# A new order for the first unit, a late q load by the software queue, and q loads behind the k transfers

## The chip, the cores and the metric

The kernel runs on one NeuronCore of a Trainium2 chip. Its engines run side by side, each with its own list of instructions: TensorE (PE; the loading of weights into it is listed as PEld), VectorE (DVE), ScalarE (ACT), GpSimd (POOL) and SyncE (SP, which here only issues transfers). An instruction waits until the semaphores of its operands have been raised; what stands behind it in the same list waits too. Transfers issued by SyncE go through a hardware queue, those issued by GpSimd through a software queue; both are carried by the same 16 DMA engines. The metric is the time of one execution on the device in microseconds (us). The kernel before takes 222.96 us, the median of 13 runs (221.85 to 223.95).

## The reference: what is computed

Sparse attention, followed by a two-layer feed-forward. There are 4 batches of 8 heads with 768 positions and a head size of 64. Each position attends to the 31 positions around it and to one summary per block of 32 positions: the largest k of the block as its key, the mean v as its value.

```python
k_sum = k.reshape(B, H, nb, block, D).max(axis=3)
v_sum = v.reshape(B, H, nb, block, D).mean(axis=3)
scores_l = where(|pos_i - pos_j| < 16, scale * q @ k.T, -1e9)
scores_s = scale * q @ k_sum.T + log(block)
a = softmax(concat([scores_l, scores_s]))
attn = a @ concat([v, v_sum])
h = x @ w_in                      # x: attn as [3072, 512]; w_in [512, 2048]
out = (h / (1 + exp(-1.702 * h))) @ w_out      # w_out [2048, 512]
```

Inputs and output are float32; the kernel computes in bfloat16 with float32 sums in PSUM.

## The kernel before

**Units.** The work is cut into 8 units `u`: a batch `b = u // 2` and half of its positions (384). A unit is attention for its half, a transposition of the result to `xT[0..3]` (one tile for each pair of heads `p`), then `ff_in` (16 column tiles `nt` of h, four matmuls each, a gelu on ACT into `gT`) and `ff_out` (3 blocks `ms` of 128 rows, each in 4 parts of 4 matmuls, copied by ACT and stored). The attention of unit u + 1 is written between the parts of ff_out of unit u: `beside(u + 1, i)` looks up in `plan`, `plan0` or `plan1` what goes to slot i (s: scores of a pair, v: values, t: transposition of q on TensorE, x: of the result on TensorE, d: of the result by a transfer).

**Order.** Every engine keeps the order in which the program writes its instructions (`_Ordered`). For the first unit, which has no ff_out to stand beside, this order is written out by hand as a list of short steps (from `cast_k(act, 0, 0)` on); the engine is an argument of most steps. For a pair p:

- `cast_k`, `cast_q` bring the float32 load to bfloat16; `k_turn`, `q_turn` transpose it on TensorE (products with `ident`) into PSUM; `k_own`, `q_copy` bring it from there to `kx` and `qT`.
- `k_max` takes the block maxima, `k_blocks` puts them into `ksz`, `k_sides` copies neighbouring keys.
- `s_turn`, `s_exp`, `s_mask` give the local weights `a_sb`; `b_turn`, `b_exp` those of the summaries (`ab`, two pairs in one tile).
- `v_own`, `v_even`, `v_before`, `v_after` put v into `vw`; `v_sum` and `v_copy` make the block sums.
- `av_near`, `av_blocks` form the values in PSUM, `v_norm` divides, `x_turn` transposes; a `copy` brings the result to `xT[p]`; `ff_first(p)` does the products of xT[p] for the first `N0 = 2` column tiles.
- `idle(n)` issues n matmuls on the constant tile `warm`, whose result nobody reads. They go to unused columns of the tile that `st["idle"]` names at that point: that of the last k_turn, s_turn, av_near or v_copy.

"dve_alone" as an engine means a copy by a reduction over an axis of length one.

**PSUM.** Two pools share its 8 banks: `pmm` (4 tiles of one bank) and `psb` (2 tiles of two banks), each handed out in turn. A tile is handed out again when the last reader of its predecessor is done.

**Queues.** SyncE first issues the loads of batch 0: k (8 transfers), the first half of q (4), v (8), the second half of q (4; "late q", first needed by `cast_q(dve, p, 1)` at the start of ff_in of unit 0, whose `q_turn(p, 1)` stand behind nt = 4 to 7). GpSimd issues the weights, cast to bfloat16 on the way, in 8 chunks: `load_w_in(0)` and `(1)` inside the list, the other six after it. In ff_out of unit 0 SyncE issues `hold`, a small transfer that reads the third w_out chunk, and behind it all loads of batch 1. Batches 2 and 3 are loaded in ff_out of units 1 and 3: k at `i == 1`, v and q at `i == 8` (i counts parts, and is raised before it is compared). In units 2 and 4 GpSimd casts the next batch; k and q are then transposed by transfers: `xk` at the start of the unit, `xq` in its ff_out at `i == 10`, followed by `halo_dmas` and `sum_dmas`, which complete `vw`.

Of the kernel before, what the change touches and what calls it, by code (L numbers as in the profile page):

```python
# [9 lines left out]
F32 = mybir.dt.float32  # L10
# [24 lines left out]
def kernel(  # L35
# [45 lines left out]
    raw = {}  # L81
# [16 lines left out]
    def load_q(b, p, half=None):  # L98
# [5 lines left out]
        t = stage.tile([128, 2, JH, D], F32, name=f"qf{p}{half}", tag=f"qf{p}{half}")  # L104
# [3 lines left out]
        raw["q", p, half] = t  # L108
# [206 lines left out]
    def idle(n):  # L315

        tile, o, start = st["idle"]
        for i in range(n):
            pe.matmul(out=tile[:, o:o + 120], lhsT=warm[:, 0:128], rhs=warm[:, 0:120],
                      start=start, stop=True, skip_group_check=True)  # L320
# [63 lines left out]
    st = {}  # L384

    def k_turn(p):
        src = cast.pop(("k", p))
        big = st["K", p] = psb.tile([128, 1024], F32, name="ps_k", tag="big")
        st["idle"] = big, 904, True
# [30 lines left out]
    def q_turn(p, half=0):  # L420
# [6 lines left out]
        for r in range(JH):  # L427
            pe.matmul(out=ps[:, r * 128:r * 128 + 128],
# [3 lines left out]
    def q_copy(p, eng, half=0):  # L432

        copy(eng, qT[p][0][:, half * HALF:half * HALF + HALF].rearrange("p (c r) -> p r c", r=JH),
             st["Q", p][:, 0:HALF].rearrange("p (r c) -> p r c", r=JH))

    def s_turn(p):
# [3 lines left out]
        st["idle"] = big, 904, True  # L441
# [28 lines left out]
    def b_exp(g):  # L470
        ab = st["ab", g] = attp.tile([128, HALF], BF16, name="ab", tag="ab")
        act.activation(out=ab, in_=st["B", g][:, 0:HALF], func=ACT.Exp, scale=scale)

# [25 lines left out]
    def v_copy(p, eng):  # L499
# [4 lines left out]
        if p == NP - 1:  # L504
            st["idle"] = st["VT"], 0, True
# [5 lines left out]
    def av_near(p):  # L511
# [11 lines left out]
        if p < 2:  # L523
            st["idle"] = st["V", p // 2], p % 2 * 512 + 392, False
# [15 lines left out]
    def x_turn(p):  # L540
        src = x_sb.pop(p)
        if p == 0:
            st["X", 0] = pmm.tile([128, 2, HALF], BF16, name="ps_x", tag="mm")
# [123 lines left out]
    N0 = 2  # L667
# [56 lines left out]
    for p in range(NP):  # L724
        load_q(0, p, 1)
# [6 lines left out]
    cast_k(act, 0, 0)  # L732
    cast_k("dve_alone", 0, 1)
    cast_k(act, 1, 1)
    cast_k(pool, 2, 1)
    cast_k(dve, 1, 0)
    k_turn(0)
    k_own(0, dve)
    cast_k(act, 2, 0)
    idle(5)  # L740
    k_turn(1)
    idle(5)
    k_turn(2)
    k_max(0)
    k_own(1, act)
    k_sides(0, dve)
    cast_k(act, 3, 0)
    k_own(2, act)
    k_blocks(0, pool)
    cast_k(dve, 3, 1)  # L750
    k_sides(1, pool)
    k_sides(2, pool)
    k_max(1)
    cast_q(pool, 2, 0)
    cast_q(act, 0, 0)
    idle(4)
    k_turn(3)
    cast_q("dve_alone", 1, 0)
    k_max(2)
    idle(2)  # L760
    q_turn(0)
    k_own(3, act)
    k_sides(3, dve)
    k_blocks(1, pool)
    q_turn(1)
    q_copy(0, act)
    cast_q(pool, 3, 0)
    q_copy(1, act)
    q_turn(2)
    k_blocks(2, pool)  # L770
    idle(3)
    b_turn(0)
    v_own(0, 0, act)
    s_turn(0)
    s_turn(1)
    v_before(0, pool)
    k_max(3)
# [240 lines left out]
```

## Time and profile before

| what | value |
|---|---|
| median of 13 runs | 222.96 us |
| the profiled execution's own time | 222.92 us |
| its span, first to last instruction | 221.2 us |
| TensorE busy | 210.6 us |
| ScalarE busy | 136.8 us |
| VectorE busy | 90.8 us |
| GpSimd busy | 67.9 us |
| moved by the DMA engines | 37.36 MB |
| first ff matmul of unit 0 | at 25.22 us |
| first w_out matmul of unit 0 | at 37.34 us |
| first load of batch 1 | at 42.36 us |

Times within the profile are counted from the first instruction. In a timeline each line gives start, length, engine, operation and names, out<-in, then how many instructions were merged and, in brackets, how long the engine had been idle and what ended that. All of the kernel's instructions carry line 27, that of the helper that records them; they are told apart by the names of their tiles: `kb`, `qb` the casts, `ps_k`, `ps_q`, `ps_s`, `ps_b`, `ps_vt`, `ps_av`, `ps_x` the PSUM tiles of the steps above, `ph` and `po` those of ff_in and ff_out. The chain of work that ended last goes back from the last instruction to what released each step.

### The profile page before, as it was taken

How to read it: one execution, taken by the hardware profiler on the slowest of the kernel's cores; microseconds unless marked ns; L12 is line 12 of the kernel's file. 1: busy time of each engine (PE TensorE's matmuls, PEld its weight loads, DVE VectorE, ACT ScalarE, POOL GpSimd, SP SyncE). 2: the span in 40 equal slices, each digit the busy share in tenths (PEclk: the TensorE clock that was granted, in tenths of full speed). 3: DMA queues.
4: the chain of work that ended last, by engine and by line, in shares of the span. 5: the costliest groups of instructions: out<-in, count | busy, mean ns of one | idle time of the engine just before them, and what ended most of it. 6: DMA issues, size and time to landing. Idle time of an engine off the chain costs nothing.

```text
span 221.2 us, 5025 instructions
## 1 busy us (share of the span) xinstructions
PE 210.6 (95%) x1989; PEld 120.0 (54%) x1989; DVE 90.8 (41%) x262; ACT 136.8 (62%) x241; POOL 67.9 (31%) x164
## 2 busy tenths in 40 slices
PE   7778999999999999999999999999999999999993
PEld 3656765456555556454655465545655564556542
DVE  5689890454984720185506200549126001700000
ACT  3488577556578747862788277845786478637420
POOL 5289983023954428610003256600000000000000
PEclk9999999999999999999999999999999999999999
DMA  5999999899999999999989999999723300340012
GB/s 167 315 217 210 216 215 217 150 235 197 252 342 199 235 207 217 224 154 185 183 171 234 207 236 210 216 165 201 140 60 95 122 0 3 83 128 5 0 47 96
DMA packets 94407, 37.36 MB, mean 169 GB/s; under 512 B 78704, under 2 KB 91440, under 8 KB 94384
## 3 DMA queue, kind: packets, MB, share of 16 engines
q1 hardware_dynamic: 90160, 32.85, 73.4%
q0 software_dynamic: 4224, 4.19, 11.6%
q8 instruction: 15, 0.25, 0.5%
q14 instruction: 8, 0.07, 0.1%
HBM read 27.26 MB, written 6.29 MB: 152 GB/s over the span
## 4 chain that ended last, share of the span: by engine, by line
PE 86%; DVE 6%; ACT 4%; issue 1%; ACTq 0%; DVEq 0%
PE po L27 37%; PE ph L27 36%; PE ps_av L27 4%; PE ps_s L27 3%; PE ps_k L27 2%; DVE kx L27 2%; PE ps_w L27 2%; ACT a_sb L27 1%; ACT kx L27 1%; DVE qT L27 1%; PE ps_q L27 1%; PE ps_x L27 1%; DVE ks L27 1%; PE ps_vt L27 1%; DVE a_sb L27 1%
## 5 line engine op out<-in xcount | busy, mean ns | idle before, releaser
L27 PE MATMUL po<-w_out_sb,gT 128*128 128x512 bf16 (+2 forms) x400 | 89.0, 371 | 0.0
L27 PE MATMUL ph<-xT,w_in_sb 128*128 128x384 bf16 x512 | 86.5, 326 | 0.9 <-DVE xT L27 0.6
L27 ACT ACTIVATE gT<-ph 128x384 bf16<-128x384 f32 x128 | 61.5, 490 | 27.5 <-PE ph L27 27.3
L27 PEld LDWEIGHTS <-w_in_sb 128*128 128x128 bf16 x512 | 49.4, 98 | 33.6 <-issue 1.7
L27 PEld LDWEIGHTS <-gT 128*128 128x128 bf16 x400 | 36.4, 98 | 38.5
L27 DVE TENSOR_TENSOR a_sb<-a_sb,mk 128x768 bf16<-128x768 bf16 x32 | 18.9, 597 | 75.1 <-ACT a_sb L27 73.8
L27 ACT ACTIVATE osb<-po 128x512 f32<-128x512 f32 (+1 forms) x24 | 14.2, 592 | 36.6 <-PE po L27 36.6
L27 ACT ACTIVATE a_sb<-ps_s 128x768 bf16<-128x768 f32 x32 | 24.3, 806 | 7.0 <-PE ps_s L27 6.5
L27 POOL CAST vw<-vf 128x768 bf16<-128x768 f32 (+3 forms) x35 | 24.2, 719 | 13.1 <-DMA vf<-in_v_dram 12.6
L27 POOL CAST kb<-kf 128x768 bf16<-128x768 f32 (+1 forms) x13 | 10.7, 820 | 48.8 <-DMA kf<-in_k_dram 48.8
L27 ACT ACT_TABLE_LOAD x16 | 20.5, 1283 | 1.1 <-PEq L1002 0.8
L27 DVE TENSOR_TENSOR x<-ps_av,rc 128x384 bf16<-128x384 f32 x28 | 15.6, 558 | 1.0
L27 POOL CAST qb<-qf 128x384 bf16<-128x384 f32 (+1 forms) x18 | 12.3, 696 | 8.2 <-DMA qf<-in_q_dram 5.6
L27 DVE TENSOR_REDUCE ks<-kx 128x24 bf16<-128x768 bf16 x12 | 11.2, 937 | 1.4 <-ACT kx L27 1.4
L27 PEld LDWEIGHTS <-a_sb 128*64 128x64 bf16 x384 | 8.0, 111 | 6.7 <-issue 3.8
L27 DVE COPY osb<-po 128x128 f32<-128x128 f32 x1 | 0.3, 292 | 24.9 <-PE po L27 24.9
L27 PE MATMUL ps_av<-vw,a_sb 128*64 128x65 bf16 x384 | 10.1, 198 | 0.2 <-DVE a_sb L27 0.2
L27 PEld LDWEIGHTS <-kx 64*128 64x128 bf16 x384 | 7.0, 95 | 4.7 <-issue 4.0
L27 PE MATMUL ps_s<-qT,kx 64*128 64x64 bf16 x384 | 9.2, 191 | 0.4 <-ACT qT L27 0.2
L27 PEld LDWEIGHTS <-warm 128*128 128x128 bf16 x71 | 6.0, 115 | 6.4 <-issue 4.8
L27 DVE COPY kx<-kx 128x80 bf16<-128x80 bf16 (+4 forms) x52 | 8.9, 223 | 0.9 <-ACT kx L27 0.9
L27 DVE CAST qT<-ps_q 128x384 bf16<-128x384 f32 (+1 forms) x8 | 7.6, 961 | 3.3 <-PE ps_q L27 3.2
(70 smaller groups left out, 119.9 us busy)
## 6 DMA issues: line engine op xcount, KB each, us to landing
out_dram<-osb SPq DMA_DIRECT2D x23, 256.0 KB, 2.3
kf<-in_k_dram SPq DMA_DIRECT2D x12, 384.0 KB, 6.6
vf<-in_v_dram SPq DMA_DIRECT2D x12, 384.0 KB, 6.8
qf<-in_q_dram SPq DMA_DIRECT2D x16, 192.0 KB, 4.3
qf<-in_q_dram SPq DMA_DIRECT2D x8, 384.0 KB, 6.2
w_in_sb<-in_moe_w_in_dram POOLq DMA_DIRECT2D x4, 512.0 KB, 9.8
w_out_sb<-in_moe_w_out_dram POOLq DMA_DIRECT2D x4, 512.0 KB, 17.8
kf<-in_k_dram SPq DMA_DIRECT2D x8, 192.0 KB, 3.8
```

The lines of the kernel that those rows point to most:

```text
L27: r = f(*a, **kw)
```

## The change

- The list of the first unit is written in another order, with other engines for many steps.
- `idle` writes 128 columns of `st["idle"]` only once that names a tile: the q tile of the last pair after its q_copy, then the second b tile after its b_exp; before, none are issued. The lines that named other tiles go. `busy` is defined and not called.
- `q_turn` for the first half writes PSUM so that `q_copy` reads it contiguously.
- `N0` is 3.
- Late q of batch 0 becomes one load for all pairs, issued by GpSimd behind the list's end, ahead of `load_w_in(2)`.
- `ff_in(u, range(3))` at the start of a unit holds for units 1 and 2 as well.
- q of batches 2 and 3 is loaded at the start of units 2 and 4, behind `xk`; v at `i == 7`.

```diff
@@ load_q
+        if half and p == 0:
+            late[0] = stage.tile([128, NP, 2, JH, D], F32, name="qfl", tag="qfl")
+            if b == 0:
+                pool.dma_start(out=late[0].rearrange("p i h r d -> p (i h) (r d)"),
+                               in_=q[0, :, HALF:S].rearrange("h (p r) d -> p h (r d)", r=JH))
+        t = (late[0][:, p] if half else
+             stage.tile([128, 2, JH, D], F32, name=f"qf{p}0", tag=f"qf{p}0"))
+        raw["q", p, half] = t
+        if b == 0 and half:
+            return
@@ idle
-        tile, o, start = st["idle"]
+        if st.get("idle") is None:
+            return
         for i in range(n):
-            pe.matmul(out=tile[:, o:o + 120], lhsT=warm[:, 0:128], rhs=warm[:, 0:120],
-                      start=start, stop=True, skip_group_check=True)
+            pe.matmul(out=st["idle"][:, 0:128], lhsT=warm[:, 0:128], rhs=warm[:, 0:128],
+                      start=True, stop=True)
@@ q_turn, q_copy
-            pe.matmul(out=ps[:, r * 128:r * 128 + 128],
+            pe.matmul(out=ps[:, r * 128:r * 128 + 128] if half else at(ps, r, [[JH, 128]]),
...
+        if half == 0:
+            copy(eng, qT[p][0][:, 0:HALF], st["Q", p][:, 0:HALF])
+            if p == NP - 1:
+                st["idle"] = st["Q", p]
+            return
@@ b_exp
+        if g:
+            st["idle"] = st["B", g]
@@ x_turn
+            if st.get("idle") is st["Q", NP - 1]:
+                st["idle"] = None
@@
-    N0 = 2
+    N0 = 3
@@ the list (new order only)
+    cast_k("dve_alone", 0, 0)
+    cast_k(dve, 0, 1)
+    cast_k(dve, 1, 0)
+    cast_k(dve, 1, 1)
+    k_turn(0)
+    cast_k(pool, 2, 1)
+    k_own(0, act)
+    k_turn(1)
+    k_sides(0, dve)
+    cast_k(act, 2, 0)
+    k_own(1, act)
+    k_turn(2)
+    k_max(0)
+    k_blocks(0, dve)
+    k_sides(1, pool)
+    cast_k(act, 3, 0)
+    k_own(2, act)
+    cast_k(dve, 3, 1)
+    k_turn(3)
+    cast_q(pool, 0, 0)
+    k_own(3, act)
+    cast_q(pool, 1, 0)
+    q_turn(0)
+    cast_q(pool, 2, 0)
+    q_copy(0, act)
+    q_turn(1)
+    k_max(1)
+    k_sides(2, pool)
+    q_turn(2)
+    k_max(2)
+    q_copy(1, act)
+    s_turn(0)
+    b_turn(0)
+    k_blocks(2, dve)
+    q_copy(2, act)
+    k_blocks(1, pool)
+    v_own(0, 0, pool)
+    b_turn(1)
+    cast_q(dve, 3, 0)
+    k_max(3)
+    v_before(0, pool)
+    v_own(0, 1, "dve_alone")
+    s_turn(2)
+    s_exp(0)
+    b_exp(0)
+    k_sides(3, pool)
+    q_turn(3)
+    s_exp(2)
+    s_turn(1)
+    v_even(0, dve)
+    s_mask(0, dve)
+    s_exp(1)
+    v_before(1, act)
+    q_copy(3, dve)
+    v_sum(0)
+    v_even(1, act)
+    v_own(1, 0, pool)
+    v_after(0, pool)
+    v_copy(0, dve)
+    b_turn(2)
+    s_turn(3)
+    v_own(1, 1, dve)
+    s_mask(2, dve)
+    idle(8)
+    v_sum(1)
+    s_mask(1, dve)
+    av_near(0)
+    v_after(1, act)
+    k_blocks(3, pool)
+    v_copy(1, act)
+    v_own(2, 0, "dve_alone")
+    av_blocks(0, 0, D + 1)
+    b_turn(3)
+    v_own(2, 1, act)
+    av_near(1)
+    load_w_in(0)
+    load_w_in(1)
+    av_blocks(1, 0, D + 1)
+    v_before(2, pool)
+    b_exp(1)
+    idle(8)
+    v_sum(2)
+    v_own(3, 0, "dve_alone")
+    v_norm(0)
+    v_after(2, pool)
+    v_own(3, 1, "dve_alone")
+    x_turn(0)
+    v_even(2, act)
+    s_exp(3)
+    idle(6)
+    v_sum(3)
+    idle(4)
+    av_near(2)
+    v_copy(2, act)
+    v_after(3, act)
+    copy(dve, xT[0], st["X", 0 // 2][:, 0 % 2])
+    v_norm(1)
+    v_before(3, pool)
+    av_blocks(2, 0, D + 1)
+    s_mask(3, dve)
+    v_even(3, pool)
+    v_copy(3, act)
+    x_turn(1)
+    idle(4)
+    av_near(3)
+    v_norm(2)
+    gelu_soon()
+    copy(act, xT[1], st["X", 1 // 2][:, 1 % 2])
+    idle(4)
+    av_blocks(3, 0, D + 1)
+    idle(8)
+    x_turn(2)
+    ff_first(0)
+    ff_first(1)
+    v_norm(3)
+    x_turn(3)
+    copy(act, xT[2], st["X", 2 // 2][:, 2 % 2])
+    ff_first(2)
+    copy(dve, xT[3], st["X", 3 // 2][:, 3 % 2])
+    ff_first(3)
+    for p in range(NP):
+        load_q(0, p, 1)
     load_w_in(2)
@@ the units
                     xk(p // 2, s)
             for p in range(NP):
+                load_q(b + 1, p)
+            for p in range(NP):
                 cast_v(pool, s, p, 0)
...
-        if u > 2:
+        if u:
             ff_in(u, range(3))
...
-            elif half and b + 2 < B and i == 8:
+            elif half and b + 2 < B and i == 7:
                 load_v(b + 2)
-                for p in range(NP):
-                    load_q(b + 2, p)
```

## The prediction, made before the change was run

> **What bounds the kernel now.** I read the page first, then the chain that ended last, the timeline of the first 45 us engine by engine, and the DMA side (windows, landings, SyncE's waits).
>
> ```profile
> span 221.2 us, 5025 instructions
> PE 210.6 (95%) x1989; PEld 120.0 (54%) x1989; DVE 90.8 (41%) x262; ACT 136.8 (62%) x241; POOL 67.9 (31%) x164
> DMA  5999999899999999999989999999723300340012
> ```
>
> TensorE is the engine that ends last; its 95% contains the idle matmuls of the first unit. The DMA row says the second thing: the transfer engines are as full as TensorE up to slice 28, some 155 us. So time can be won only where TensorE waits, and only as far as the transfers come earlier too. The chain (start, length, what):
>
> ```profile
> 26.76 2.93 PE ph L27 x18
> 32.30 5.20 PE ph L27 x32
> 51.02 0.57 DVE xT L27
> 79.35 0.57 DVE xT L27
> 79.96 10.25 PE ph L27 x62
> ```
>
> From 26.8 us on it is TensorE with short holes; the holes are the copies of xT at 51.0 and 79.4, and the part before 26.8, where the chain changes engine more than twenty times. The timeline of TensorE shows why the first part is slow (in brackets: idle before, and what ended it):
>
> ```profile
> 7.19 0.66 PE L27 MATMUL ps_k<-warm 128*128 128x120 bf16 x5 [1.05 <-DVE kx L27]
> 7.64 1.48 PE L27 MATMUL ps_k<-ident,kb 128*128 128x128 bf16 x6
> 9.43 1.39 PE L27 MATMUL ps_k<-ident,kb 128*128 128x128 bf16 x6
> 11.71 0.37 PE L27 MATMUL ps_k<-warm 128*128 128x120 bf16 x4 [0.90 <-ACT kx L27]
> 11.92 0.82 PE L27 MATMUL ps_k<-ident,kb 128*128 128x128 bf16 x6
> 21.56 0.52 PE L27 MATMUL ps_vt<-vw,E 128*64 128x128 bf16 x6 [0.44 <-DVE vs L27]
> 26.60 3.09 PE L27 MATMUL ph<-xT,w_in_sb 128*128 128x384 bf16 x18
> ```
>
> Matmuls on `warm`, which compute nothing, wait for the reader of the tile that they write into, and the next transposes of k stand behind them. The first unit's input to the feed-forward is complete at 26.60 + 6 x 0.1625 = **27.57** (end of ff_first(3)). Beside it the transfers:
>
> ```profile
> 6.00:9.00 3.00, 1.95 (x13) 1.81 (x12) 2.47 (x5) 1.04 (x2) 0.86 (x3) 1.00 1.05 337
> 18.00:21.00 3.00, 2.64 (x59) 1.99 (x56) 2.74 (x9) 3.00 (x8) 2.94 (x6) 1.00 1.05 187
> 25.00:30.00 5.00, 4.71 (x41) 3.21 (x40) 4.42 (x25) 2.63 (x7) 4.39 (x16) 1.00 1.24 207
> SPq L27 <- DMA w_out_sb<-in_moe_w_out_dram: 10.2, 1, 10.2
> ```
>
> (Last three columns of a window: clock, DMA share, GB/s.) Plain 768-byte rows run at 337 GB/s, casting weight chunks at 207, and where late q and w_in share the engines only 187. The eight weight chunks land at 25.1, 27.7, 30.2, 33.6, 36.6, 39.1, 41.7, 44.2 (issue plus landing time of each), 2.53 us apart where nothing else moves. TensorE asks for them at 25.2, 28.4, 32.1, 34.7, 37.3, about 40.5 and 44.0 (first use in the timeline): only 0.1 to 2.3 us later. The last line is the `hold` transfer: all loads of batch 1 wait for the seventh chunk, and SyncE then issues without a pause up to 74.35. So the second batch starts with the weights, not with TensorE.
>
> **The change, part by part.**
>
> **The new order of the first unit.** I gave each step the length of its row (k_own 0.81 on ACT, k_max 0.95, casts 0.36 on DVE, 0.50 on POOL, s_exp 0.8, s_mask 0.56, v_norm 0.76, ff 0.1625 a matmul; instructions of ACT and DVE that follow each other overlap by about 0.1), let each engine run its own list, and let each step wait for its operands, its PSUM bank and the landing of its input. Put through this, the old order ends ff_first(3) at 27.64 against 27.57 in the trace, the first w_in issue at 15.72 against 15.66, and the fourth v_sum at 21.44 against 21.56. The new order gives:
>
> - k_turn(0) to (3) end at 5.9, 7.5, 8.9 and 10.25 (old: 5.9, 8.9, 10.6, 12.8). Nothing but casts and landings of k holds them.
> - q_turn now writes PSUM in steps of three, as k_turn does, at k_turn's 0.109 a matmul in place of 0.056: +0.16 each. q_copy becomes contiguous: 0.49 (ACT, as a 128x384 gelu) for 0.73. q_copy(0) ends at 11.7 instead of 14.3.
> - Scores, exps and masks follow on a full ACT; b_exp(1) ends at 17.1. The new wait is idle(8) on it: behind it on TensorE stand v_sum(2) and x_turn(0), 0.2 us of wait.
> - From 17.5 on landings of v rule: v_own(3,0) waits for its load at 17.5, then v_norm(0) 18.8, xT[0] 19.65, v_norm(1) 20.3, s_mask(3) 20.8, av_blocks(3) 21.9, v_norm(3) 22.9, xT[2] and xT[3] 24.4, ff_first(3) **25.43**.
>
> That is 2.2 earlier. ff_first now carries three column tiles (N0 = 3), so another 4 x 0.1625 = 0.65 of later work is done by then.
>
> [...] Before 13.9 us 19 idle matmuls go. The rows show what is at stake: six transposes take 1.48 at 7.64 and 0.82 at 11.92, though the page's PEclk prints 9 throughout. [...] I take 25.55: **-2.0, with N0 -2.65**; by the strict rule, full windows alone, -2.5 (bounds -1.15 and -2.8).
>
> **Late q and the weights.** Four SyncE loads (14.80 to 17.18; behind them on SyncE nothing until the halos at 26.4) become one GpSimd load behind load_w_in(1). Both w_in issues move up: GpSimd reaches them at 15.2 and 16.0 (old 15.66, 18.39). [...] The row: the issue beside an s_mask took 0.88, the others 0.74. [...] I take the row.
> An SP load of 192 KB lands 3.6 after issue at best, of which 0.6 is its transfer at 337 GB/s: 3.0 fixed, my estimate for these too. Two chunks unshared would have landed at 15.66 + 3.0 + 5.06 = 23.7; they did at 27.7. New: 15.3 + 3.0 + 5.06 = 23.4. Then late q, 786 KB: 2.3 at 337 GB/s, 3.8 at 207; the software queue has shown only casting chunks, so I take the middle, 3.0: lands at 26.4. w_in(2) follows at 28.9 instead of 30.2, and all that follows is **1.3 to 1.4 earlier** (bounds 0.5 and 2.1), if GpSimd issues late q (at about 19.2, behind v_even(3)) in time. Behind it on GpSimd: six weight issues, the v casts, vrows0 with the halos, the masks for 40 us: all with 3 us or more to spare.
> The new wait is cast_q(dve, p, 1) on late q: DVE is there at 26.2 after the key halos, TensorE wants the first q_turn at 26.8; landing at 26.4 plus a 0.4 cast just serves. At 27.2 it costs 0.8 of TensorE, behind which the whole feed-forward stands; the weights would hide half of it.
>
> **ff_in in threes for units 1 and 2.** The hole behind the xT copies (0.3 and 0.3 after the first two matmuls) is filled with the other tiles' first halves; the second tile's bank waits for an output copy of 0.6. Worth 0.3 and 0.4 at most, nothing if something later limits.
>
> **q of batches 2 and 3 behind the k transposes.** Four loads each are moved on SyncE past the store of the third output block and four kx transposes; behind them now stand the next store and the two xT transposes that TensorE needs at 103.88 (and 150.84).
>
> ```profile
> 83.12 7.06 SPq L27 DMA_DIRECT2D qf<-in_q_dram  x4
> 92.06 6.99 SPq L27 DMA_TRANSPOSE kx<-kb  x4
> 99.95 3.21 SPq L27 DMA_TRANSPOSE xT<-x  x2
> ```
>
> Same transfers, same queue, other order: 7.06 and 6.99 swap, so the xT transposes keep their place near 99.95: 0. Bounds: -1 (TensorE not held at all) to +2.9 (rival). load_v at i == 7 for 8 passes the second block's store (issue at 77.46, 0.53): the v loads start up to 0.6 earlier, the store some 5 later, and its buffer is wanted only one unit later: 0, since what follows is served in order.
>
> **The sum.** TensorE by itself would be 2.65 + 0.3 earlier by unit 2. But the first w_out chunk, at 36.6 - 1.4 = 35.2, is asked for at 37.3 - 2.65 = 34.7: of 2.65 some 2.1 pass. And the batch-1 loads, with SyncE's list up to 74.35, are 1.4 earlier; at 74.92 SyncE waits 0.57 for x, so that much slack is there: 1.4 + 0.6 = **2.0** passes, the smallest of the three. 222.92 (the profiled execution's own time, 221.2 of span and 1.7 around it; the median of the 13 runs is 222.96) - 2.0 = **220.9**.
>
> **Rivals.**
> 1. *The weights gain little* (late q at the slow rate, or descriptors delayed): seventh chunk 0.5 earlier, end 1.0 earlier: 221.9. For: 187 GB/s when the two queues share. Against: afterwards nothing shares.
> [...]
> 3. *Slower: xT behind q.* q loads land 6.2 after issue. If the last issue ends where kx did (99.05, begun 97.35), it lands at 103.55, the xT transpose 1.6 later at 105.2: TensorE waits 1.4 in unit 3, 1.5 in unit 5 (146.26 by the same steps). 2.9 against 2.0: 223.8. It decides from 1.0 us a place. For: the second of those xT transfers starts at about 101.6, is used at 104.9, and the median one needs 2.8 to land. Against: a queue served in order delivers the same bytes by the same time.
>
> **How the numbers follow.** Likeliest 0.45 (own range 219.9 to 221.5), rival 1 0.20 (221.5 to 222.3), rival 2 0.13, rival 3 0.22 (223.6 to 225). About 0.3% (0.67 us) is what a measurement can tell here. Faster 0.65, same 0.13, slower 0.22. The range runs from 219.4 (clock early, late q at 337 GB/s) to 224.2, inside rival 3; left out is its upper half and a little below.
>
> **What would show it.** ff_first(3) ending at 25.4 to 25.7 (27 means the clock); no kx wait before warm matmuls; w_in issues near 15.3 and 16; seventh chunk at 40.3 (41.2 is rival 1); no wait of ff matmuls for xT near 102 and 149 (1.4 each is rival 3). A first feed-forward that waits for qb would prove late q too late.

## The result: slower, and the profile after

The changed kernel takes 225.69 us (median), the kernel before 222.72 us beside it: a ratio of **1.0131** (95% interval 1.0108 to 1.0155), 3.0 us slower where 2.0 us faster was forecast. The profiled execution of the changed kernel took 224.58 us, with a span of 222.9; that is 1.7 over the profiled execution of the kernel before (222.92), so the profiles show only a part of the 3.0. One thing has to be known to read the times: a ratio leaves out executions more than 1.5% above the fastest of their kernel, while executions that lost TensorE clock can be on either side of that line. Of 13 listed executions of the changed kernel, 10 have a mean granted clock under 0.9965 and a median of 226.3, the other three a median of 224.7; of 217 listed executions of the kernel before, 29 have such a mean.

The timeline of TensorE in the changed kernel (start, length, operation, count, in brackets the idle time before and what ended it), where the feed-forward of the first unit begins:

```profile
24.01 1.14 PE L27 MATMUL ph<-xT,w_in_sb 128*128 128x384 bf16 x6
24.99 0.33 PE L27 MATMUL ps_x<-ident,x_sb 128*128 128x128 bf16 x3
25.89 2.44 PE L27 MATMUL ph<-xT,w_in_sb 128*128 128x384 bf16 x14 [0.58 <-ACT xT L27]
30.45 0.34 PE L27 MATMUL ps_q<-ident,qb 128*128 128x128 bf16 x3 [2.12 <-DVE qb L27]
31.61 1.49 PE L27 MATMUL ph<-xT,w_in_sb 128*128 128x384 bf16 x4
33.21 1.49 PE L27 MATMUL ph<-xT,w_in_sb 128*128 128x384 bf16 x4
```

Of the 14 matmuls at 25.89 the first six are ff_first(2) and (3), so ff_first(3) ends at 25.89 + 6 x 0.1625 = 26.87: 0.7 earlier than in the profile before, not 2.0 (and the 0.7 is owed to a slow start of that one profile, as the part on the prediction shows). At 28.33 TensorE stops for 2.12 us: the first late q_turn waits for the cast of late q. After it, four feed-forward matmuls take 1.49 where they took 0.81 before. The windows (the last three columns are granted clock, transfer engines' busy share, GB/s) show why, and show a second thing at 15 to 20 us; the first line is the kernel before, the others are the changed kernel:

```profile
15.00:20.00 5.00, 4.48 (x92) 3.32 (x88) 4.65 (x11) 5.00 (x12) 4.76 (x10) 1.00 1.14 215
15.00:20.00 5.00, 4.06 (x79) 3.35 (x80) 4.28 (x12) 4.01 (x9) 4.43 (x9) 1.00 0.68 115
...
31.00:32.00 1.00, 1.00 (x8) 0.69 (x7) 1.00 (x4) 0.46 (x1) 0.80 (x4) 0.63 1.23 194
32.00:33.00 1.00, 1.00 (x6) 0.50 (x4) 0.66 (x2) 0.03 (x1) 0.78 (x5) 0.50 1.03 113
33.00:34.00 1.00, 1.00 (x7) 0.66 (x6) 0.54 (x1) 0.49 (x1) 0.87 (x5) 0.50 1.16 202
34.00:35.00 1.00, 1.00 (x8) 0.60 (x7) 0.30 (x2) 0.26 (x1) 0.89 (x5) 0.67 1.18 226
```

The granted clock is one half from about 31.26 (0.63 of that microsecond is 0.26 at full and 0.74 at half) to 34.66, which is 3.40 us. And between 15 and 20 us the transfer engines move 115 GB/s, where they moved 215 before: from 17 to 19 us they are nearly idle (shares of 0.11 and 0.19), because late q no longer comes from SyncE and the weights are not there yet. GpSimd's timeline shows why they are not:

```profile
13.81 1.27 POOL L27 COPY kx<-kx 128x192 bf16<-128x192 bf16 x2
15.04 1.12 POOL L27 CAST vw<-vf 128x384 bf16<-128x384 f32 x2
16.12 0.99 POOL L27 COPY ksz<-ks 64x24 bf16<-64x24 bf16 x2
17.06 1.63 POOL L27 DMA_DIRECT2D w_in_sb<-in_moe_w_in_dram  x2
...
21.07 0.90 POOL L27 DMA_DIRECT2D qfl<-in_q_dram  x1
```

The first w_in is issued at 17.06 (forecast 15.2), late q at 21.07 (forecast 19.2), and the chain of waits counts 8.94 us from there to its landing at 30.0. The weights then land at 22.6, 25.1, 32.4, 35.7, 38.8, 41.3, 43.9 and 46.4 (issue plus landing time of each). From the third on that is 2.2 later than before. SyncE, with the hold of the kernel before in the first line, and then the chain of the changed kernel:

```profile
41.71 0.61 SPq L27 DMA_DIRECT2D hold<-w_out_sb  x1
...
43.93 0.61 SPq L27 DMA_DIRECT2D hold<-w_out_sb  x1
44.59 5.05 SPq L27 DMA_DIRECT2D kf<-in_k_dram  x4
...
76.89 1.38 SPq L27 DMA_TRANSPOSE xT<-x  x1
```

```profile
21.07 8.94 DMA qfl<-in_q_dram
...
76.89 5.32 DMA xT<-x
82.25 10.57 PE ph L27 x64
```

TensorE where the feed-forward of unit 2 begins, before (two lines) and changed:

```profile
79.15 0.49 PE L27 MATMUL ph<-xT,w_in_sb 128*128 128x384 bf16 x2
79.96 10.24 PE L27 MATMUL ph<-xT,w_in_sb 128*128 128x384 bf16 x62 [0.32 <-DVE xT L27]
...
82.25 10.57 PE L27 MATMUL ph<-xT,w_in_sb 128*128 128x384 bf16 x64 [1.45 <-DMA xT<-x]
```

The hold goes at 43.93 instead of 41.71 (+2.2). The feed-forward of unit 2 starts at 82.25 instead of 79.15 (+3.1), is through 2.6 later (in threes it has no hole behind its first matmuls), and the last block of the kernel starts at 209.39 instead of 207.37 (+2.0). Between unit 2 and the end nothing more is lost in this profile.

So two explanations stand against each other. **Theory W**: TensorE's wait of 2.12 and the half clock after it (1.7 of work) are the loss. **Theory T**: the transfers are: the weights land 2.2 later, the seventh chunk releases batch 1, SyncE's list runs without a pause from there to the transpose of x for unit 2, and TensorE has time to wait (1.45 at 82.25). Both have the right size.

### The profile page after: what moved, and what is told of

Same layout as the page of the kernel before. It is cut to its first block, busy times and chain, and to the rows that moved or that the text cites. A ratio compares the mean times of both kernels' runs of the same rounds, so it can differ in the third digit from the quotient of the medians.

```text
span 222.9 us, 4964 instructions
## 1 busy us (share of the span) xinstructions
PE 209.8 (94%) x1968; PEld 116.9 (52%) x1968; DVE 89.9 (40%) x261; ACT 136.4 (61%) x242; POOL 70.2 (31%) x165
## 4 chain that ended last, share of the span: by engine, by line
PE 82%; DMA 9%; SPq 3%; issue 2%; ACT 1%; POOL 1%; DVE 1%; ACTq 0%; DVEq 0%; POOLq 0%
PE ph L27 37%; PE po L27 36%; DMA qfl<-in_q_dram 4%; PE ps_av L27 3%; PE ps_s L27 3%; SPq L27 3%; DMA vf<-in_v_dram 3%; DMA xT<-x 2%; PE ps_q L27 1%; POOL vw L27 1%; DVE qT L27 1%; PE ps_vs L27 1%; PE ps_t L27 1%; ACT vw L27 0%; ACT a_sb L27 0%
## 5 line engine op out<-in xcount | busy, mean ns | idle before, releaser
L27 PE MATMUL ph<-xT,w_in_sb 128*128 128x384 bf16 x512 | 87.6, 329 | 2.0 <-DMA xT<-x 1.4
L27 PEld LDWEIGHTS <-w_in_sb 128*128 128x128 bf16 x512 | 49.9, 99 | 34.8 <-DMA xT<-x 1.6
L27 DVE TENSOR_TENSOR a_sb<-a_sb,mk 128x768 bf16<-128x768 bf16 x32 | 19.2, 606 | 75.7 <-ACT a_sb L27 74.5
L27 POOL CAST vw<-vf 128x768 bf16<-128x768 f32 (+4 forms) x36 | 25.0, 720 | 12.4 <-DMA vf<-in_v_dram 11.3
L27 POOL CAST qb<-qf 128x768 bf16<-128x768 f32 (+1 forms) x15 | 10.6, 709 | 21.8 <-DMA qf<-in_q_dram 19.8
L27 DVE COPY kx<-kx 128x80 bf16<-128x80 bf16 (+4 forms) x50 | 9.4, 242 | 0.0
L27 DVE RECIPROCAL rc<-ps_av 128x6 f32<-128x6 f32 x32 | 6.1, 190 | 7.4 <-PE ps_av L27 7.3
L27 DVE CAST qT<-ps_q 128x384 bf16<-128x384 f32 (+1 forms) x7 | 6.5, 946 | 4.6 <-PE ps_q L27 4.6
```

Source lines behind the costliest of these rows:

```text
L27: r = f(*a, **kw)
```

## Experiments

All ratios are against the kernel before measured alongside, with 95% intervals; times in the text are from one profiled execution of each kernel.

**Late q by SyncE again.** load_q as before, its four calls behind load_v(0), the rest as changed.

```diff
     load_v(0)
+    for p in range(NP):
+        load_q(0, p, 1)
     hold = consts.tile([16, 16], BF16, name="hold")
```

> The changed kernel with late q issued by SyncE behind v again, everything else as changed. Theory W (TensorE's 2.1 us wait for qb at 30.45 and the halved clock of 31 to 35 us that follows are the loss): no wait for qb, ff without a hole, 2.1 + 1.9 less, about 221.5. Theory T (late q stands in the queue of the weights and the transfer engines lie idle from 17 to 19 us, so the chunks from the third on land 2.2 us later than before, and the seventh chunk releases batch 1): the gap at 17 is filled, the third chunk lands at about 30.4 instead of 32.4, the hold goes at about 41.9 instead of 43.9, about 223.0. Both theories: faster than the changed kernel.

Measured: **1.0035** (1.0008 to 1.0062). Most of the loss comes back, as both theories had it, but the median of 224.35 is above both of their times (221.5 and 223.0). The hold went at 40.70, unit 2 started at 79.14. One line of TensorE's timeline was in neither theory:

```profile
29.01 0.34 PE L27 MATMUL ps_q<-ident,qb 128*128 128x128 bf16 x3 [0.72 <-DVE qb L27]
```

Late q had landed by then, and TensorE still waits 0.72 for its cast: VectorE stands in the key halos, which run from 26.11 to 28.66 here and from 26.15 to 29.07 in the changed kernel.

**TensorE's wait taken away, the queue left as it is.**

```diff
-                todo[4 + p] = [lambda p=p: (q_turn(p, 1), q_copy(p, dve, 1))]
+                todo[8 + p] = [lambda p=p: (q_turn(p, 1), q_copy(p, dve, 1))]
```

> The changed kernel with the late q_turn and q_copy at feed-forward tiles 8 to 11 instead of 4 to 7; the loads stay. This takes TensorE's wait for qb away and leaves the queue of transfers as it is. Theory W: 2.5 to 4 us less than the changed kernel, 221.7 to 223.2. Theory T: the third chunk still lands at 32.4 and the seventh at 43.9; TensorE waits for w_in instead of qb, batch 1 starts no earlier, time as the changed kernel within 0.5, about 225.5.

Measured: **1.0113** (1.0061 to 1.0166, from six executions). About 0.2% came back, with intervals that allow more; theory W had 1.1 to 1.8%, 221.7 to 223.2 us, and the lowest of the six took 224.51. In its profile (TensorE, then SyncE) the wait has moved to the weights, the clock stays at 1.00, and the hold is nearly as late as in the changed kernel:

```profile
26.14 4.38 PE L27 MATMUL ph<-xT,w_in_sb 128*128 128x384 bf16 x26 [0.58 <-ACT xT L27]
32.16 0.82 PE L27 MATMUL ph<-xT,w_in_sb 128*128 128x384 bf16 x4 [1.64 <-DMA w_in_sb<-in_moe_w_in_dram]
```

```profile
43.08 0.61 SPq L27 DMA_DIRECT2D hold<-w_out_sb  x1
```

Its span is 222.9, the same as that of the changed kernel; unit 2 starts 1.1 earlier, with the hold 0.85 earlier, and loses it again in three waits for masks (0.38, 0.16, 0.28). TensorE waits 1.91 for the transpose of x at unit 2 here, and 1.45 in the changed kernel. So in the profiled execution of the changed kernel the wait for qb and the half clock after it were hidden, and theory W, as an account of that execution, falls.

**Late q first in the queue.** The late load ahead of load_w_in(0) and load_w_in(1) on GpSimd.

```diff
+    for p in range(NP):
+        load_q(0, p, 1)
     load_w_in(0)
     load_w_in(1)
```

> The changed kernel with GpSimd's late q issued at once ahead of w_in(0) and w_in(1) instead of behind them; the queue carries the same bytes ahead of the third chunk. Theory W: qb is there at about 22.5, no wait for it, w_in(0) lands at about 24.5 where ff_first wants it at 24.0, about 222. Theory T: third chunk at about 32.3, seventh at 43.8, as in the changed kernel: 225 to 226.

Measured: **1.0090** (1.0057 to 1.0122). Late q landed at 23.0 and nobody waited for qb; the third chunk landed at 30.9 and the seventh at 42.4, earlier than I had put for theory T (43.8) and later than before. TensorE now waited 1.44 for w_in(0) and then ran at half clock for 6.8 us. Theory W's 222 did not come. The median, 225.81, is theory T's number, but with a hold that went 1.55 earlier than in the changed kernel; the lost clock is a part of it.

**Late q alone, in the old order.** The software-queue load of late q behind load_w_in(1) put into the kernel before.

> The kernel before with late q alone put on the software queue behind w_in(1), as in the change; old order of the first unit, old q loads. Late q is issued at about 20.0 and lands at about 27, ahead of its q_turn at 29.5. Theory W: no wait, 222.7 as before. Theory T: the transfer engines have less to do between 17 and 18.5 us, and the third chunk lands 0.3 to 1.2 us later than 30.2: 223.0 to 223.9.

Measured: **1.0050** (1.0025 to 1.0074), median 224.07, a little over theory T's range. Here late q landed at 27.6 and the third chunk at 30.2, no later than before, against theory T; the seventh landed at 42.2, 0.5 later. Unit 2 starts 0.3 later (79.49), and later in the profile TensorE waits 0.33, 0.25 and 0.40 for VectorE, where the kernel before has one wait of 0.15. So moving late q costs in the old order too, but less, and not by the third chunk.

**The q loads of batches 2 and 3 alone**, in the kernel before.

> The kernel before with the q loads of batches 2 and 3 alone moved behind the k transfers (and v one place earlier). Theory T (the transfers and SyncE's list decide up to unit 2, later loads are hidden): the same as before within 0.3%, 222.4 to 223.7. A rival, that the moved loads cost the loss: slower by 1 or more.

Measured: **1.0005** (0.9985 to 1.0026). The moved loads cost nothing.

**The order alone.** Late q by SyncE and the old q loads; left are the order of the first unit, N0 = 3, q_turn's steps and the threes.

> The changed kernel with late q by SyncE behind v and the q loads of batches 2 and 3 where they were: what is left of the change is the order of the first unit, N0 = 3, q_turn's steps of three and the feed-forwards of units 1 and 2 in threes. Prediction's reckoning of the order: 2 or more faster than before, 220.7. Theory T: the weights leave only about 1 (the seventh chunk at 40.7 as with late q by SyncE in the run before), 222.0 to 223.2. The difference to the run with late q by SyncE alone (1.0035 of before) is the price of the moved q loads.

Measured: **1.0035** (1.0016 to 1.0055). Not the prediction's 2 us faster, nor theory T's 222.0 to 223.2, but 0.8 us slower. The seventh chunk landed at 42.1.

**Batch 1 released one chunk earlier**, in the changed kernel.

```diff
-                sp.dma_start(out=hold, in_=w_out_sb[0:16, NT - 5, 0:16])
+                sp.dma_start(out=hold, in_=w_out_sb[0:16, NT - 9, 0:16])
```

> The changed kernel with the hold transfer reading the second chunk of w_out instead of the third, so that SyncE's loads of batch 1 start when the sixth chunk of weights lands and not the seventh. Theory T: SyncE's list starts about 2.4 earlier (41.5 instead of 43.9) and ends as much earlier; the last two chunks then share the engines and land up to 2 later, which first TensorE feels; 1.0 to 2.4 faster than the changed kernel, 223.3 to 224.7. Theory W (TensorE's wait decides): no change, 225.7.

Measured: **1.0058** (1.0023 to 1.0094), 0.73% or 1.6 us back, while TensorE's wait for qb is still there (1.9). The hold went at 40.65 and unit 2 started at 80.24 instead of 82.25. This is theory T's gain, and theory W had none. In the profile only 0.4 of the 2.0 is left at the last block: TensorE waits four times for masks in between, 1.26 in all, and the profile of the changed kernel has no such wait (the last section shows one).

**The wait filled.** 38 matmuls on warm ahead of the first late q_turn.

```diff
-                todo[4 + p] = [lambda p=p: (q_turn(p, 1), q_copy(p, dve, 1))]
+                todo[4 + p] = [lambda p=p: (p or busy(38), q_turn(p, 1),
+                                            q_copy(p, dve, 1))]
```

> The changed kernel with 38 matmuls on warm put ahead of the first late q_turn, so that TensorE works through its wait for qb (28.3 to 30.4) and the clock gate has nothing to act on. Theory W: without the halved clock 1.9 less, 223.8. Theory T for the profiled execution: no gain, since the seventh chunk lands at 43.9 all the same. In the times of the changed kernel those executions with a mean clock under 0.993 are about 1.6 longer than the others: if this wait is where their clock falls, they are gone and the median is about 224.7.

Measured: **1.0050** (1.0026 to 1.0073). 4 of 11 executions still lost clock and took 226.3 to 228.9; the ratio is that of the other seven, so it flatters this kernel. The median of all eleven is 224.38 (224.7 was named), 1.3 below the changed kernel's 225.69. By transfers alone there was no gain to come (the seventh chunk still landed at 43.9), so this points to the clock as a loss of its own in the times. Where the clock fell in executions that were not profiled is not on record. The profiled one is one of the four (TensorE, then windows):

```profile
82.23 12.25 PE L27 MATMUL ph<-xT,w_in_sb 128*128 128x384 bf16 x64 [2.54 <-DMA xT<-x]
```

```profile
83.00:84.00 1.00, 1.00 (x6) 0.54 (x4) 0.00 (x0) 0.00 (x0) 0.00 (x0) 0.60 1.39 223
84.00:85.00 1.00, 1.00 (x5) 0.46 (x4) 0.00 (x0) 0.75 (x2) 0.80 (x2) 0.50 1.38 216
85.00:86.00 1.00, 1.00 (x5) 0.45 (x3) 0.00 (x0) 0.72 (x2) 0.82 (x3) 0.50 1.39 219
86.00:87.00 1.00, 1.00 (x5) 0.50 (x4) 0.00 (x0) 0.34 (x1) 1.00 (x2) 0.69 1.39 218
```

The filled TensorE reaches unit 2 sooner, waits 2.54 there for the late transpose of x, and loses the clock behind that wait instead. There it is on the path: 64 matmuls take 12.25 instead of 10.57. The late release makes the second hole, late q the first.

**Both mended.** The fill and the earlier release together.

> The changed kernel with both the 38 matmuls in the wait for qb and the hold on the second chunk of w_out. Singly they gave 1.0050 and 1.0058 of before, the changed kernel 1.0131. If the clock and the late release are two separate losses, the gains add up: 0.998 to 1.001. If both only mend the same loss: about 1.005.

Measured: **1.0027** (1.0005 to 1.0048); 2 of 22 executions lost clock. The changed kernel's 1.31% becomes 0.27%: what the two take back together is 1.04%, each alone 0.7 to 0.8%. That they overlap, as holes that feed each other would, is likely but not shown: the intervals are too wide to tell 1.04% from the sum.

**The kernel before, released earlier** (second chunk of w_out, then the first).

> The kernel before with the hold transfer reading the second chunk of w_out instead of the third, nothing else. Theory T: SyncE's list of batch 1 starts about 2.5 earlier (39.2 instead of 41.7), the transpose of x for unit 2 is issued earlier, but TensorE itself reached unit 2 only 0.3 before its x: the gain there ends at 0.3 to 0.9, and the last two chunks of w_out land later beside the loads; 221.8 to 223.0.

> The kernel before with the hold on the first chunk of w_out, 2.5 us earlier again than on the second. TensorE reached unit 2 with only 0.24 of wait in the run with the second chunk, so earlier loads of batch 1 have nothing left to give there, while three chunks of w_out now land beside them: 0.998 to 1.004, no better than 0.9973.

Measured: **0.9973** (0.9951 to 0.9994) and **0.9964** (0.9946 to 0.9983). The release was late in the kernel before already. The first chunk was to be no better than the second; it is at least as good. Unit 2 started at 77.77 and 77.79, 1.4 earlier than before, where 0.3 to 0.9 was expected of the second chunk (the 0.3 was the hole behind the first two matmuls, a wait for a copy of xT and not for the transfer).

**The changed kernel with late q by SyncE, released earlier.**

> The changed kernel with late q by SyncE and the hold on the second chunk of w_out. Here TensorE waits 1.47 at 79.14 for the transfer of x in the run with late q by SyncE alone. Theory T: this wait goes, up to 1.5 faster than that run (1.0035 of before): 221.5 to 223.0. If the new order itself loses time, no gain, 223.5 and more.

Measured: **1.0000** (0.9975 to 1.0025): 0.35% better than without, of the 0.62% that would have made it as good as the old order with the same release (0.9973). The median of 223.55 misses theory T's 221.5 to 223.0.

**GpSimd beside VectorE.** In the changed kernel s_mask(0), (1), (2) as a three-operand instruction, v_even(0) and v_own(1,1) as reductions.

```diff
-    v_even(0, dve)
+    v_even(0, "dve_alone")
...
-        eng.tensor_mul(a, a, m)
+            eng.scalar_tensor_tensor(out=a, in0=a, scalar=1.0, in1=m,
+                                     op0=ALU.mult, op1=ALU.mult)
```

> The changed kernel with the first three s_masks on VectorE as a three-operand instruction and v_even(0) and v_own(1,1) as reductions, so that no plain VectorE copy, cast or product of two bf16 tiles stands beside GpSimd's k_sides(3) and k_blocks(3). [...] The time by theory T follows the chunks: 0.5 to 1 less than the changed kernel, unless the slower masks hold TensorE.

Measured: **1.0174** (1.0123 to 1.0225), the opposite of the expectation. These are four executions, with an interval that overlaps the changed kernel's; what speaks is the profile. GpSimd, then VectorE:

```profile
14.32 1.81 POOL L27 COPY kx<-kx 128x192 bf16<-128x192 bf16 x2
...
16.98 1.86 POOL L27 COPY ksz<-ks 64x24 bf16<-64x24 bf16 x2
18.79 1.63 POOL L27 DMA_DIRECT2D w_in_sb<-in_moe_w_in_dram  x2
```

```profile
14.69 0.95 DVE L27 SCALAR_TENSOR_TENSOR a_sb<-a_sb,mk 128x768 bf16<-128x768 bf16 x1
...
16.95 1.82 DVE L27 SCALAR_TENSOR_TENSOR a_sb<-a_sb,mk 128x768 bf16<-128x768 bf16 x2
```

Two copies of 24 columns, 0.40 at their shortest, take 1.86 for as long as two masks take 1.82; in the changed kernel they take 0.99 beside two masks of 1.33. The two kx copies take 1.81 here beside a mask of 0.95, and 1.27 in the changed kernel beside one of 0.54. With longer masks GpSimd's copies were longer. w_in(0) is now issued at 18.79, in the changed kernel at 17.06.

**Order of the first unit or threes?** The order alone without the threes, and the kernel before with the threes alone.

> The changed kernel with late q by SyncE, the q loads of batches 2 and 3 where they were, and units 1 and 2 with one column tile at a time as before: only the order of the first unit, N0 = 3 and q_turn's steps of three are left of the change. The run with the threes was 1.0035 of before. If the threes are what costs, 0.999 to 1.001 here; if the order of the first unit does, 1.003 to 1.004 again. My prediction's reckoning of the order would be 0.99.

> The kernel before with the feed-forwards of units 1 and 2 in threes, nothing else. The prediction had 0.3 and 0.4 us at most for it: 0.997 to 1.0. If the threes are what costs in the run with the order alone: 1.003.

Measured: **1.0046** (1.0020 to 1.0072) and **0.9984** (0.9960 to 1.0009). The threes cost nothing and may give the little that was forecast; the loss is the order's (with N0 = 3 and q_turn's steps).

**Two combinations of the old order**: hold on the second chunk with the moved q loads; hold on the first chunk with the threes.

> The kernel before with the hold on the second chunk of w_out and the q loads of batches 2 and 3 behind the k transfers. The hold alone gave 0.9973, the q loads alone 1.0005 with intervals of 0.002. If both are independent: 0.997 to 0.998.

> The kernel before with the hold on the first chunk of w_out and the feed-forwards of units 1 and 2 in threes. Singly 0.9964 and 0.9984. If both gains are separate: 0.994 to 0.996, faster than both kernels.

Measured: **0.9983** (0.9958 to 1.0009) and **0.9967** (0.9939 to 0.9994). The second is faster than both kernels, but not by more than the hold on the first chunk alone, which is the version to keep.

**The new order, freed.** Late q by SyncE, its casts ahead of the key halos, hold on the first chunk.

```diff
+    for p in range(NP):
+        cast_q(dve, p, 1)
     for p in range(NP):
         key_halos(p, 0, dve, JH)
```

> The changed kernel with what was found in its way taken out: late q by SyncE, the four late casts of q ahead of the key halos on VectorE (which hold the first late q_turn by 0.7 in the run with late q by SyncE), the hold on the first chunk of w_out. Against the run of the kernel before with the same hold and the same threes it differs by the order of the first unit, N0 = 3, q_turn's steps and the moved q loads. If the new order is worth the 2 us of the prediction once nothing else is late: 0.988 or less. If the landing of w_in(0) (23.9 to 25.1) and the transfers leave it nothing: no faster than the other run of this call, 0.995 to 1.0.

Measured: **1.0013** (0.9978 to 1.0049), against 0.9967 for the old order measured with it. The first late q_turn no longer waits. But its first lines are these:

```profile
24.57 1.15 PE L27 MATMUL ph<-xT,w_in_sb 128*128 128x384 bf16 x6 [0.34 <-DMA w_in_sb<-in_moe_w_in_dram]
25.56 0.33 PE L27 MATMUL ps_x<-ident,x_sb 128*128 128x128 bf16 x3
26.46 2.44 PE L27 MATMUL ph<-xT,w_in_sb 128*128 128x384 bf16 x14 [0.58 <-ACT xT L27]
```

ff_first(0) waits for w_in(0), x_turn(3) stands behind it on TensorE, and ff_first(3) ends at 26.46 + 6 x 0.1625 = 27.44, against 27.57 in the profile of the kernel before. Freed of all else, the new order gives TensorE 0.13 there, and comes later than most profiles of the old order (26.37 to 26.73, see below).

**What ties the runs together** is the time from the hold to unit 2, that is to the first feed-forward matmul of unit 2:

| kernel | hold goes | unit 2 starts | between | ratio |
|---|---|---|---|---|
| late q by SyncE | 40.70 | 79.14 | 38.4 | 1.0035 |
| before, q loads moved | 40.85 | 78.48 | 37.6 | 1.0005 |
| before, threes | 40.86 | 78.08 | 37.2 | 0.9984 |
| order without threes | 41.61 | 80.72 | 39.1 | 1.0046 |
| before | 41.71 | 79.15 | 37.4 | 1 |
| order alone | 42.15 | 80.08 | 37.9 | 1.0035 |
| before, late q soft | 42.17 | 79.49 | 37.3 | 1.0050 |
| late q first | 42.38 | 81.48 | 39.1 | 1.0090 |
| late q_turn later | 43.08 | 81.19 | 38.1 | 1.0113 |
| changed | 43.93 | 82.25 | 38.3 | 1.0131 |
| wait filled | 43.93 | 82.23 | 38.3 | 1.0050 |
| masks in three operands | 44.78 | 82.87 | 38.1 | 1.0174 |
| changed, hold on second | 40.65 | 80.24 | 39.6 | 1.0058 |
| both mended | 40.80 | 80.06 | 39.3 | 1.0027 |
| late q by SyncE, hold on second | 40.06 | 79.84 | 39.8 | 1.0000 |
| before, hold on second | 38.18 | 77.77 | 39.6 | 0.9973 |
| before, hold on second, q loads moved | 38.08 | 78.79 | 40.7 | 0.9983 |
| order freed, hold on first | 35.75 | 78.09 | 42.3 | 1.0013 |
| before, hold on first, threes | 35.48 | 78.48 | 43.0 | 0.9967 |
| before, hold on first | 35.52 | 77.79 | 42.3 | 0.9964 |

In the first twelve rows the hold moves by 4.1 us and the distance stays within 37.2 to 39.1, whatever TensorE did in the first unit. In the other eight, with the release out of the way, the distance grows to between 39.3 and 43.0. The ratio goes along with the start of unit 2: the changed kernel is 3.1 us later there than the kernel before and 2.9 slower, the hold on the first chunk 1.4 earlier and 0.8 faster. It does so within about 1.4 us (the wait filled apart), and small steps in the table mean nothing: three kernels with the same code up to the hold (the kernel before as it is, with the q loads moved, and with threes) have it at 40.85 to 41.71, three others (late q by SyncE, the order alone, the order without threes) at 40.70 to 42.15.

## Why the prediction was wrong, step by step

**Late q and the weights** is the step that failed, in its sign: "all that follows is 1.3 to 1.4 earlier (bounds 0.5 and 2.1)" measured 2.2 later. Two terms were mis-sized. w_in(0) was issued 1.9 late (17.06 for 15.2), so w_in(1) landed 1.7 late (25.1 for 23.4), and late q took 4.9 behind it (to 30.0), not 3.0; together that is about the 3.5 by which the third chunk missed its forecast (32.4 for 28.9). By the packet record, from 27 to 28 us w_in(2) already moves 139 packets (of 1024 bytes) beside 11 of late q (of 4608), so some of the 16 engines seem to have been still at late q while the others had gone on. These two turn 1.3 earlier into 2.2 later. What the forecast did not ask stands behind them: taking late q out of SyncE's queue does not take its bytes away. It left the transfer engines nearly idle from 17 to 19 us (shares of 0.11 and 0.19) and put the same 786 KB ahead of the third chunk. An unshared queue was counted as a gain without asking what the vacated time was filled with. The observation named as proof of late q too late, a first feed-forward that waits for qb, is the line at 30.45.

**GpSimd beside VectorE** was weighed by the wrong row. The row chosen (an issue beside an s_mask took 0.88, not 0.74) tells of issues, and 0.1 was taken from it (15.3 for 15.2). GpSimd's copies stretch: k_sides(3) 1.27 for 0.64, one v_after cast 0.67 for 0.50, the two ksz copies 0.94 for 0.40, together 1.34 of the 1.86 by which w_in(0) came late. VectorE has a mask beside the first (14.05 to 14.59, with casts around it) and two beside the last (15.72 to 17.05). In the run with three-operand masks the two pairs of copies take 1.81 and 1.86 (1.27 and 0.99 in the changed kernel), and all but the last 0.07 of the second pair lies beside the two masks, which take 1.82 there: it is the masks that they go with. 0.1 taken, 1.3 measured.

**cast_q's wait**: "DVE is there at 26.2 after the key halos" is the forecast xT[3] at 24.4 and the 1.8 that the halos take in the kernel before (27.07 to 28.90). But xT[3] came at 26.24, and the halos then took 2.9, to 29.07. VectorE (one group of halos before, then two in the changed kernel) and GpSimd in the changed kernel:

```profile
27.99 0.35 DVE L27 COPY kx<-kx 128x48 bf16<-128x48 bf16 x3
...
26.51 0.96 DVE L27 COPY kx<-kx 128x48 bf16<-128x48 bf16 x3
27.50 0.93 DVE L27 COPY kx<-kx 128x48 bf16<-128x48 bf16 x3
...
26.36 2.02 POOL L27 CAST vw<-vf 128x384 bf16<-128x384 f32 x4
```

Three copies of 48 columns take 0.93 to 0.96 beside GpSimd's v casts and 0.32 to 0.43 in the kernel before, whose halos come after those casts (24.54 to 26.39). In the runs with late q by SyncE and with the order alone only the first group meets the casts, and only that one is long (1.09 and 1.07). The late halos alone make the 0.72 in the run with late q by SyncE; the other 1.4 of the 2.12 is the landing at 30.0.

**The order of the first unit**: forecast 25.55 for ff_first(3), measured 26.87, and the 27.57 that both are held against is not how the old order usually runs. Eight profiles have the old list. In five of them TensorE turns k at full pace from the second pair on, as here in the kernel before with threes:

```profile
7.43 0.82 PE L27 MATMUL ps_k<-ident,kb 128*128 128x128 bf16 x6
8.35 0.82 PE L27 MATMUL ps_k<-ident,kb 128*128 128x128 bf16 x6
25.56 3.09 PE L27 MATMUL ph<-xT,w_in_sb 128*128 128x384 bf16 x18
```

In the profile that the prediction started from, the same transposes take 1.48 and 1.39, at nearly half the pace, though the windows print a clock of 1.00 there. The five end ff_first(3) at 26.37 to 26.73, the other three at 27.57 to 27.63. So about 1.0 of the forecast 2.0 (an estimate, 27.57 less 26.5) was the late clock of one execution, which most profiles of the old order do not have. The new order ends ff_first(3) at 26.56 to 27.12 where late q stands behind w_in(1) and the masks are as they were, and at 26.83 to 28.42 with late q by SyncE. By then it has done 0.65 of matmuls that the old order does later (N0 = 3). Counting these, it is a few tenths ahead with late q behind w_in(1), and on average half a microsecond behind with late q by SyncE.

Where the walk went wrong can be followed. Up to v_norm(0) the walk held (18.8 forecast, 18.88 measured). But k_blocks(3) is one of the copies that GpSimd did late, so b_exp(1) ended at 18.53 instead of 17.1, and the idle matmuls on its bank held TensorE for 0.60, not 0.2. Then v_norm(2) stands between av_near(3) and av_blocks(3) in program order, and pairs 2 and 3 share a PSUM tile: v_norm(2) waited 0.84 for av_near(3), av_blocks(3) 0.56 for v_norm(2) and came at 23.21 instead of 21.9. In the same way a tile shared by xT[2] and xT[3] made the copy of xT[2] wait for x_turn(3), which stood behind six ff_first matmuls. The walk had dependencies by operand and bank, not by tile. N0 = 3 shortened the later work as worked out, but it adds to what waits for w_in(0): once late q is back on SyncE and shares the engines, w_in(0) lands at 23.9 to 25.5, and that is the new bound.

**The clock**: nothing was lost in the first transposes of the changed kernel's profile (three transposes of k take 0.50 from 5.8 us on, as at 8.6); it was the profile of the kernel before that had the clock late. No run shows the 0.12 by which the forecast's 25.55 exceeds the walk's 25.43, nor the -2.5 and the bounds beside it: they were my estimates. In place of the -2.0 built on them, the profiles of the changed kernel and of the kernel before are 0.7 apart at ff_first(3) (26.87 and 27.57). The clock fell elsewhere. In the four profiles where it fell ahead of TensorE's last matmul, the 3.4 us before the fall, about as long as the shortest fall itself, hold 1.8 (order alone), 1.8 (late q first), 2.1 (changed) and 2.4 us (wait filled) of TensorE's holes, in one or several. Single holes passed of 1.91 and 1.64 (late q_turn later) and of 1.45 (changed, at unit 2), so the length of a hole alone does not decide.

**The sum** was built rightly: SyncE's list from the seventh chunk to unit 2 was the smallest of three gains in the prediction, and it is what the table shows. With +2.2 in place of -1.4 and no other change it would have said 222.92 + 2.2 = 225.1, against 224.58 profiled.

**ff_in in threes** (0.3 and 0.4 at most): 0.16% measured for both, not told from nothing. **The q loads** (0): 0.05% in the kernel before. Rival 3, the rival on the slower side, did not occur: no feed-forward of units 3 or 5 waits for xT in the changed kernel. Rival 1 names what did act (late q at 30.0 for 26.4, w_in(0) issued at 17.06 for 15.2), but as a smaller gain; no rival but the third ended behind the old kernel.

**Left open.** The order alone is 0.35 to 0.46% slower, 0.8 to 1.0 us. Its profiles point the same way: with late q by SyncE, unit 2 starts at 79.14 to 80.72, and with the old order and the same release at 78.08, 78.48 and (late clock) 79.15; the distance from the hold is 37.9 to 39.1 against 37.2 to 37.6. SyncE takes 33.2 to 33.6 from the hold to the transpose of x in both; what is longer is the time from there to the first matmul, 4.4 to 5.6 against 4.1 to 4.2. Why is not known. Freed, the order is 0.46% behind the old one (intervals of 0.3 to 0.4%), and there the profile does not show it: it took 221.25, the shortest of its 12, with a median of 224.09. Lost clock does not explain it (1 of 12). I do not know what the longer executions do.

## What to carry to other kernels

A load that is moved to another queue takes its bytes along: ask what the transfer engines do in the time it leaves, and what now lands behind it. When one transfer releases the next stage, measure the distance from that release to the stage's start; if it stays the same while the compute engine moves, time won on that engine ahead of it is only waiting, and the release itself is the thing to move. A hole in TensorE can cost twice, once as a wait and once as clock, or nothing: here one of 2.12, with 3.40 us at half clock behind it, was hidden at 31 us in the changed kernel, and one of 2.54, with 3.42 behind it, was on the path at 83 us in the filled one. And take more than one profile of the kernel that you want to beat: two executions of the same first unit differ by 1 us at its end, and half of the 2.0 forecast for the order was counted from the slower one.

## What the hardware showed that I had not expected

Where the clock fell it fell to one half, and for nearly the same time: 3.40 us in the changed kernel, 3.42 behind the wait for x (83.20 to 86.62), 3.42 in the order alone (11.16 to 14.58), and twice that, 6.8, with late q first. Such a stretch at half clock is 3.41 x 0.5 / 222 = 0.8% of the span, so a mean clock of about 0.992 in a listed execution would be one stretch and 0.985 two (an estimate): eight and two of the 13 executions of the changed kernel. The first rise differs too: the trace's clock record begins, at full clock, at 10.59 us in the profile of the kernel before and at 3.94 in that of the changed kernel. In the eight profiles of the old first unit the windows from 7 to 9 us count 15 matmuls in the three that end ff_first(3) at 27.57 to 27.63, and 25 in the other five.

VectorE's masks are longer beside GpSimd, too: two of them took 1.64 beside a cast of q in a later unit, and TensorE waited 0.38 for the second. The timeline of late q by SyncE (GpSimd, VectorE, TensorE):

```profile
95.50 1.64 DVE L27 TENSOR_TENSOR a_sb<-a_sb,mk 128x768 bf16<-128x768 bf16 x2
95.72 1.02 POOL L27 CAST qb<-qf 128x768 bf16<-128x768 f32 x1 [7.86 <-DMA qf<-in_q_dram]
...
97.20 0.38 PE L27 MATMUL ps_av<-vw,a_sb 128*64 128x65 bf16 x12 [0.38 <-DVE a_sb L27]
```

Where the cast came 1.3 earlier, ahead of the masks (94.42 to 95.25), as in the kernel before with the q loads moved, the two masks took 1.15 and nobody waited. When q lands seems to decide it, so a few tenths come and go from run to run in units 2 to 5: such waits sum to nothing in the profile of the changed kernel and to 1.26 in that with the hold on the second chunk.
